# Scans that read one operand from PSUM, and products moved from VectorE to GpSimd, in a chunked linear attention with a routed expert stage

## The chip, the cores and the metric

The kernel runs on one core of one Trainium2 chip. The metric is the device time of one execution in microseconds. Its profile is of one execution; TensorE's clock there is given as a share of full speed, 2.4 GHz, so 0.50 is its lower level of 1.2 GHz.

## The reference, cut to what matters

A linear attention with a decaying state (4 batches, 8 heads, 768 steps, 48 dimensions) feeds a mixture of 8 experts over 3072 tokens of 384 values, each token going to the expert with the largest logit.

```python
for t in range(S):
    kt, vt, rt, wt = (k[:, :, t], v[:, :, t], r[:, :, t], w[:, :, t])
    cur = np.einsum('bhd,bhe->bhde', u[None] * kt, vt)
    y[:, :, t] = np.einsum('bhd,bhde->bhe', rt, state + cur)
    state = wt[:, :, :, None] * state + np.einsum('bhd,bhe->bhde', kt, vt)
...
x = y.transpose(0, 2, 1, 3).reshape(B * S, H * D)
logits = x @ w_gate
expert_idx = np.argmax(logits, axis=1)
...
    h = np.maximum(xe @ w1[e], 0.0)
    ye = h @ w2[e]
    out[mask] = gate_w[mask, None] * ye
```

## The kernel before

The first stage is the attention. Its 3072 tokens are 24 blocks: block n holds the 128 steps of chunk c of batch b, with n = 4c + b. Head pairs lie on 112 partitions (48 + 16 + 48), four pairs along the columns. `iteration(n)` (L739) runs for n = -3 to 21, and a hand-written end does blocks 22 and 23. Nothing reorders the instructions: each engine executes them as they are written, so an instruction that waits holds up all behind it on its engine.

One iteration has for a steady block n:

- **VectorE**: the running products of the decays forwards (`pre`, L367) and backwards (`suf`, L376) of block n+2, each one scan over four head pairs of 130 columns, 520 in all. Both multiply and add, and their added operand is an SBUF tile, `first` or `suf0`, that is zero but at the first column of each pair. Between them `reciprocal` (L370) writes the start of the backward scan. Then the products `rh` = r times pre (L349) and `kh` = k times suf (L385). `at` (L391) is two predicated copies of block n's scores from PSUM over the causal part of a tile that holds the diagonal.
- **GpSimd**: `rk` = r times k of block n+3 (L339; the first three blocks' on VectorE), held back by a dependency on the scan `pre` of block n+2; one diagonal of block n+1 (L355); and, from block 7 on, the indirect DMAs `xs<-xr,pi` (L679), four per chunk, that scatter 128 rows each to the expert that they are routed to. Their row numbers `pi` (L596) have three buffers.
- **TensorE**: the scores `ap` (L489), the state's part `yp<-rh,sst` (L501, from n = 4 on), the coefficients `cp` (L453, L456), transposes (L526, L480), the coefficients' transpose `yq<-pick,cs` (L461), the state `st` (L510), the values `yp<-at,vt` (L519).
- **ScalarE**: the copy of yp (`ytb`, in two halves L411 for the first four blocks, then in one L407), the state (L400), seven diagonals of block n+1 (L361), the coefficients `cs` of block n+2 (L422) that TensorE's L461 waits for, and smaller copies (L418, L440, L427, L396). L396 writes the carried decay into `first`.

Once per chunk there are also VectorE's gate (`mx`, `sh`, `oh`), a rank on TensorE, the exponentials on ScalarE and the count `seen` on GpSimd (L557). SyncE issues the loads; `rkwt` holds decays, r and k of a block (772 KB, six buffers).

`keep_warm(t, n)` (L118) issues n matmuls that nothing reads: 40 small and 12 wide ones at the start, 8 wide ones ahead of the coefficients of each of the first four blocks.

The second stage is the experts, sorted by size; `CAPS` are their padded row counts, in that order, in three or four groups of columns for the matmuls of L298 and in the last expert two groups of 128 rows and a rest. `Part` objects `pa` and `pb` are two halves of the first expert, computed while the attention ends; `mm1` expands, `mm2` contracts, `split_piece` and `feed` make the high and low parts of the next expert's weights, `load_x` starts a load of the next expert's rows `xg`.

Of the kernel before, what the change touches and what calls it, by code (L numbers as in the profile page):

```python
# [19 lines left out]
P = 128  # L20
# [5 lines left out]
WP = C + 2  # L26
NW = NP_ * WP
# [4 lines left out]
CAPS = (464, 440, 432, 408, 396, 384, 378, 360)  # L32
# [9 lines left out]
G0 = 2.0 ** 75  # L42
GMIN = 1e-28
# [3 lines left out]
BANK = 512  # L47
XC = DM + 2
# [4 lines left out]
def rwkv_moe_kernel(ctx, tc, rkw, vv, ub, wgp, wg, w1, w2, wc, out):  # L53
# [26 lines left out]
    def load(n):  # L80
# [9 lines left out]
        else:  # L90
# [3 lines left out]
            w=t[:, 0:NW], r=t[:, NW:NW + NR].rearrange("p (q c) -> p q c", c=C),  # L94
# [17 lines left out]
    wz = const.tile([P, BANK], BF16, name="wz")  # L112
# [222 lines left out]
    def mul_rk(n, eng):  # L335
        if real(n):
            d = blk[n]
            d["rk"] = wk.tile([RP, NP_, C], F32, name="rk", tag="rk", bufs=4)
            i = eng.tensor_tensor(out=d["rk"], in0=d["r"], in1=d["k"], op=ALU.mult)  # L339
            if real(n - 3):  # L340

                tc.add_manual_dep(i.ins, blk[n - 1]["prei"].name, mybir.DependencyInfo(
                    mybir.DependencyClass.Sync, mybir.DependencyReason.DATA), reason="beside the copies of the causal part")

    def dve_rh(n):
        if real(n):
# [16 lines left out]
    def dve_pre(n):  # L363
        if real(n):
            d = blk[n]
            pre = wk.tile([RP, NW], F32, name="pre", tag="pre")
            d["prei"] = nc.vector.tensor_tensor_scan(out=pre, data0=d["w"], data1=first[n % B].rearrange("p q c -> p (q c)"),  # L367
                                                     initial=0.0, op0=ALU.mult, op1=ALU.add).ins
            d["pre"] = pre.rearrange("p (q c) -> p q c", c=WP)
            d["rc"] = nc.vector.reciprocal(suf0[n % 2][:, :, WP - 1:WP], d["pre"][:, :, C:C + 1]).ins  # L370

    def dve_suf(n):
        if real(n):
            d = blk[n]
            suf = wk.tile([RP, NW], F32, name="suf", tag="suf")
            nc.vector.tensor_tensor_scan(out=suf[:, ::-1], data0=d["w"][:, ::-1],  # L376
                                         data1=suf0[n % 2].rearrange("p q c -> p (q c)")[:, ::-1],
                                         initial=0.0, op0=ALU.mult, op1=ALU.add)
            d["suf"] = suf.rearrange("p (q c) -> p q c", c=WP)
# [149 lines left out]
    def gate(k):  # L529
# [7 lines left out]
        nc.vector.tensor_single_scalar(out=oh, in_=sh, scalar=0.0, op=ALU.is_equal)  # L537
# [50 lines left out]
    def place(k):  # L588
# [5 lines left out]
        pi = sm.tile([P, B], I32, name="pi", tag="pi", bufs=3)[:, 0:m]  # L594
# [106 lines left out]
    class Part:  # L701
        def __init__(self, row, rows, t):
# [36 lines left out]
    def iteration(n):  # L739
# [40 lines left out]
        pe_y(n - 1)  # L780
        pe_kt(n + 1)
# [13 lines left out]
        if n == -1:  # L795
            mul_rk(2, nc.vector)
# [150 lines left out]
    with tc.manual_schedule(engines={ET.PE, ET.DVE, ET.Activation, ET.Pool}):  # L947
        for n in range(-3, NB - 2):
# [324 lines left out]
```

## Time and profile before

| | |
|---|---|
| median of the runs | 393.9 us (393.6 to 395.92, 3 runs) |
| the profiled execution | 394.28 us, of which the span is 392.5 |
| mean granted clock of TensorE | 0.989 |
| busy in the span | TensorE 373.4 us, VectorE 285.9, ScalarE 206.3, GpSimd 106.2 |

The span runs from the first to the last instruction, and what the execution has beyond it is 1.78 us. An engine that is busy 95% of the span on the mean can still wait in one stage, so the shares are read stage by stage. In rows of instructions "x2" means two of a kind in one row, and the bracket at the end is the idle time before them and what ended it.

### The profile page before, as it was taken

How to read it: one execution, taken by the hardware profiler on the slowest of the kernel's cores; microseconds unless marked ns; L12 is line 12 of the kernel's file. 1: busy time of each engine (PE TensorE's matmuls, PEld its weight loads, DVE VectorE, ACT ScalarE, POOL GpSimd, SP SyncE). 2: the span in 40 equal slices, each digit the busy share in tenths (PEclk: the TensorE clock that was granted, in tenths of full speed). 3: DMA queues.
4: the chain of work that ended last, by engine and by line, in shares of the span. 5: the costliest groups of instructions: out<-in, count | busy, mean ns of one | idle time of the engine just before them, and what ended most of it. 6: DMA issues, size and time to landing. Idle time of an engine off the chain costs nothing.

```text
span 392.5 us, 9368 instructions
## 1 busy us (share of the span) xinstructions
PE 373.4 (95%) x3545; PEld 339.8 (87%) x3548; DVE 285.9 (73%) x560; ACT 206.3 (53%) x559; POOL 106.2 (27%) x163
## 2 busy tenths in 40 slices
PE   8988999999999897999999999999999999999991
PEld 6567888878887777998999999999999999999991
DVE  7998999999999966888694693686693772722310
ACT  4788877877777655485443542463453541511200
POOL 2243256554656244111100330300240402102021
PEclk9999999999999899999999999999999999999997
DMA  8999868686706893499474475565366434001010
GB/s 287 407 304 286 254 218 262 203 253 186 251 28 169 301 306 134 139 282 265 138 227 160 125 258 186 161 193 217 120 190 214 128 114 155 21 0 46 11 37 24
DMA packets 32998, 71.25 MB, mean 182 GB/s; under 512 B 3972, under 2 KB 20229, under 8 KB 32946
## 3 DMA queue, kind: packets, MB, share of 16 engines
q1 hardware_dynamic: 29298, 61.11, 49.8%
q0 software_dynamic: 3648, 9.47, 6.6%
q8 instruction: 30, 0.49, 0.5%
q14 instruction: 22, 0.18, 0.1%
HBM read 58.73 MB, written 12.13 MB: 181 GB/s over the span
## 4 chain that ended last, share of the span: by engine, by line
PE 53%; DMA 2%; DVE 1%; issue 1%; ACT 1%; POOL 0%; POOLq 0%; SPq 0%; ACTq 0%; DVEq 0%
PE bank L298 23%; PE bank L921 14%; PE opt L315 12%; PE pt L289 2%; DMA xg<-xs 2%; PE op L910 1%; DVE w1l L235 1%; ACT w1h L233 0%; POOL out_dram L259 0%; DVE ot L911 0%; DVE ort L320 0%; ACT oT L928 0%; POOLq L1070 0%; DVE x L291 0%; ACT x L290 0%
## 5 line engine op out<-in xcount | busy, mean ns | idle before, releaser
L298 PE MATMUL bank<-xl,w1h 128*128 128x440 f32 (+6 forms) x168 | 58.2, 347 | 0.0
L298 PE MATMUL bank<-xh,w1l 128*128 128x440 f32 (+6 forms) x168 | 57.9, 344 | 0.0
L298 PE MATMUL bank<-xh,w1h 128*128 128x440 f32 (+6 forms) x168 | 55.4, 351 | 0.0
L361 ACT ACTIVATE at<-ident,cl 128x128 f32<-128x128 f32 x168 | 51.6, 392 | 0.0
L259 POOL DMA_INDIRECT out_dram<-ot,xg x16 | 21.3, 1332 | 103.2 <-DVE ot L911 99.5
L235 DVE TENSOR_TENSOR w2l<-wst,w2h 128x512 fp32r<-128x512 f32 x42 | 27.6, 687 | 24.6 <-ACT w2h L233 21.2
L300 ACT ACTIVATE hh<-bank 128x256 fp32r<-128x256 f32 (+8 forms) x58 | 26.7, 470 | 34.5 <-PE bank L298 31.5
L339 POOL TENSOR_TENSOR rk<-rkwt 112x512 f32<-112x512 f32 x21 | 27.1, 1289 | 56.3 <-DVE pre L367 49.5
L301 DVE SCALAR_TENSOR_TENSOR hl<-bank,hh 128x256 fp32r<-128x256 f32 (+8 forms) x58 | 30.0, 529 | 13.4 <-ACT hh L300 12.2
L259 POOL DMA_INDIRECT out_dram<-ort,xg x13 | 13.6, 1043 | 91.4 <-DVE ort L320 91.1
L391 DVE COPY_PREDICATED at<-cmask,ap 128x512 f32<-128x512 int32 x48 | 32.8, 740 | 1.3 <-PE ap L489 1.2
L298 PEld LDWEIGHTS bank<-xh,w1l 128*128 128x128 f32 x168 | 31.6, 188 | 0.5
L298 PEld LDWEIGHTS bank<-xl,w1h 128*128 128x128 f32 x168 | 31.6, 188 | 0.5
L233 ACT ACTIVATE w2h<-wst 128x512 fp32r<-128x512 f32 x42 | 24.5, 625 | 14.2 <-PE bank L921 10.0
L679 POOL DMA_INDIRECT xs<-xr,pi x24 | 27.5, 1147 | 16.2 <-DVE kh L385 3.4
L298 PEld LDWEIGHTS bank<-xh,w1h 128*128 128x128 f32 x168 | 31.4, 188 | 0.5
L367 DVE TENSOR_TENSOR_SCAN pre<-rkwt,first 112x520 f32<-112x520 f32 x24 | 29.6, 1233 | 0.9 <-DMA rkwt<-in_rkw_dram 0.9
L376 DVE TENSOR_TENSOR_SCAN suf<-rkwt,suf 112x520 f32<-112x520 f32 x24 | 29.9, 1244 | 0.0
L235 DVE TENSOR_TENSOR w1l<-wst,w1h 128x512 fp32r<-128x512 f32 x42 | 27.6, 687 | 1.7 <-ACT w1h L233 1.7
L489 PE MATMUL ap<-rh,kh 64*128 64x128 f32 (+1 forms) x384 | 28.4, 289 | 0.0
L315 PE MATMUL opt<-w2h,hh 128*128 128x384 f32 (+2 forms) x82 | 27.8, 345 | 0.0
L315 PE MATMUL opt<-w2h,hl 128*128 128x384 f32 (+2 forms) x82 | 27.7, 338 | 0.0
(168 smaller groups left out, 871.6 us busy)
## 6 DMA issues: line engine op xcount, KB each, us to landing
rkwt<-in_rkw_dram SPq DMA_DIRECT2D x23, 772.0 KB
wst<-in_w_dram SPq DMA_DIRECT2D x42, 256.0 KB
wst<-in_w_dram SPq DMA_DIRECT2D x14, 768.0 KB
vt<-in_vv_dram SPq DMA_DIRECT2D x24, 192.0 KB
wct<-in_wc_dram SPq DMA_DIRECT2D x24, 192.0 KB
xg<-xs SPq DMA_DIRECT2D x5, 579.0 KB
xs<-zrow SPq DMA_DIRECT2D x8, 289.5 KB
wsp<-in_w_dram SPq DMA_DIRECT2D x6, 256.0 KB
```

Of the source, the lines that this page charges most:

```text
L235: nc.vector.tensor_tensor(out=lo, in0=st[:, cs], in1=hi.bitcast(F32), op=ALU.subtract)
L259: i = nc.gpsimd.indirect_dma_start(out=out[:, :], out_offset=bass.IndirectOffsetOnAxis(ap=t.bitcast(I32)[:, q, DM + 1:DM + 2], axis=0), in ...
L298: nc.tensor.matmul(hp, a, x[:, j, :], start=(i == 0), stop=(i == 8))
L301: nc.vector.scalar_tensor_tensor(out=hl, in0=hp, scalar=0.0, in1=hh.bitcast(F32), op0=ALU.max, op1=ALU.subtract)
L315: nc.tensor.matmul(op, a[:, cs], w2v(wt, w, f), start=(i == 0), stop=(i == 23))
L361: nc.scalar.activation(blk[n]["at"][:, j, q], ident, AF.Copy, scale=blk[n]["ct"][:, 2 * q + j:2 * q + j + 1])
L367: d["prei"] = nc.vector.tensor_tensor_scan(out=pre, data0=d["w"], data1=first[n % B].rearrange("p q c -> p (q c)"), initial=0.0, op0=ALU.m ...
L376: nc.vector.tensor_tensor_scan(out=suf[:, ::-1], data0=d["w"][:, ::-1], data1=suf0[n % 2].rearrange("p q c -> p (q c)")[:, ::-1], initial= ...
L391: d["atc"] = nc.vector.copy_predicated(out=d["at"][:, j], mask=cmask.unsqueeze(1).broadcast_to([P, NP_, C]), data=d["ap"][j]).ins
L489: nc.tensor.matmul(d["ap"][j][:, q, :], d["kh"][rs, q, :], d["rh"][rs, q, :], start=True, stop=True)
L679: i = nc.gpsimd.indirect_dma_start(out=xsf, out_offset=bass.IndirectOffsetOnAxis(ap=ch["pi", c, b], axis=0), in_=xr[:, b, :], in_offset=No ...
L921: nc.tensor.matmul(pp, w, a, start=(i == 0), stop=(i == 23))
```

## The change

- The scans multiply and take a maximum. The second operand is one column of a PSUM bank that holds 2^-100, read for all columns (`floor`). The start of each pair now lies in the decays' own tile: a pair has 133 columns, 2^100, the start, 128 decays, the reciprocal, 2^100, so a scan has 533 columns. The tiles `first` and `suf0` and their memsets go.
- `rh` and every `rk` are GpSimd's. `rk` waits for the last `kh` issued (or the gate's `oh`), and not for `pre`. `rh` stands behind the diagonal and a scatter.
- The carried decay goes to `gend` on ScalarE, and a GpSimd copy of 112x4 (`pool_wt`) brings it into the decays' tile.
- On VectorE `at` stands ahead of `pre`. On ScalarE `cs` stands between the fourth and the fifth diagonal, and the exponentials behind them. `weigh` is later.
- The warm matmuls ahead of the coefficients: 6 for block 1, none for blocks 0, 2 and 3.
- `pi` has eight buffers.
- In the end of the attention, the splits of the second expert's weights and `load_x(1)` are written ahead of the two `pa.mm2`.
- The last cap is 368 for 360.

```diff
-WP = C + 2
-NW = NP_ * WP
+WP = C + 5
+NW = NP_ * WP + 4
...
-CAPS = (464, 440, 432, 408, 396, 384, 378, 360)
+CAPS = (464, 440, 432, 408, 396, 384, 378, 368)
...
+    for t in sacc:
+        nc.vector.memset(t[:RP, SC:SC + 1], 1.0 / UP)
+
+    def floor(n):
+        return sacc[n % B // 2][:RP, SC:SC + 1].broadcast_to([RP, NS])
...
-            if real(n - 3):
-
-                tc.add_manual_dep(i.ins, blk[n - 1]["prei"].name, mybir.DependencyInfo(
-                    mybir.DependencyClass.Sync, mybir.DependencyReason.DATA), reason="beside the copies of the causal part")
-
-    def dve_rh(n):
+            i = nc.gpsimd.tensor_tensor(out=d["rk"], in0=d["r"], in1=d["k"], op=ALU.mult)
+            if "behind" in ch:
+                tc.add_manual_dep(i.ins, ch.pop("behind").name, mybir.DependencyInfo(
+                    mybir.DependencyClass.Sync, mybir.DependencyReason.DATA), reason="not beside two inputs from SBUF")
+
+    def pool_rh(n):
...
-            d["prei"] = nc.vector.tensor_tensor_scan(out=pre, data0=d["w"], data1=first[n % B].rearrange("p q c -> p (q c)"),
-                                                     initial=0.0, op0=ALU.mult, op1=ALU.add).ins
-            d["pre"] = pre.rearrange("p (q c) -> p q c", c=WP)
-            d["rc"] = nc.vector.reciprocal(suf0[n % 2][:, :, WP - 1:WP], d["pre"][:, :, C:C + 1]).ins
+            nc.vector.tensor_tensor_scan(out=pre[:, 0:NS], data0=d["w"], data1=floor(n), initial=0.0, op0=ALU.mult, op1=ALU.max)
+            d["pre"] = pre[:, 0:NP_ * WP].rearrange("p (q c) -> p q c", c=WP)
+            nc.vector.reciprocal(d["wq"][:, :, C + 3:C + 4], d["pre"][:, :, C + 2:C + 3])
...
+    def pool_wt(n):
+        if real(n) and n >= B:
+            nc.gpsimd.tensor_copy(blk[n]["wq"][:, :, 2:3], gend[:, n % B, :].unsqueeze(2))
...
-        keep_warm(t, 8 if n < B else 0)
+        keep_warm(t, 6 if n == 1 else 0)
...
-        pi = sm.tile([P, B], I32, name="pi", tag="pi", bufs=3)[:, 0:m]
+        pi = sm.tile([P, B], I32, name="pi", tag="pi", bufs=8)[:, 0:m]
...
-        pa.mm2(0)
         split_piece(wts[1], stg[1, 0], 0)
         feed(1, 1, False)
-        pa.mm2(1, {f: [lambda j=j: pb.trans(j)] for j, f in enumerate((0, 2, 4))})
         split_piece(wts[1], stg[1, 1], 1)
         feed(1, 2, False)
         load_x(1)
+        pa.mm2(0)
+        pa.mm2(1, {f: [lambda j=j: pb.trans(j)] for j, f in enumerate((0, 2, 4))})
```

In the rows that follow, a scan is called SCALAR_TENSOR_TENSOR, and names are those of the code. VectorE, one iteration of the attention and the gate behind it, before:

```order
L367 SCALAR_TENSOR_TENSOR pre<-rkwt,first_165 112x520
L370 RECIPROCAL suf_0_176<-pre 112x4
L391 COPY_PREDICATED at<-cmask,ap 128x512 x2
L349 TENSOR_TENSOR rh<-rkwt,pre 112x512
L376 SCALAR_TENSOR_TENSOR suf<-rkwt,suf_0_176 112x520
L385 TENSOR_TENSOR kh<-rkwt,suf 112x512
L533 TENSOR_REDUCE mx<-cl 128x4
L535 TENSOR_TENSOR sh<-cl,mx 128x32
L537 TENSOR_SCALAR oh<-sh 128x32
```

The same place on VectorE in the changed kernel, where `st` is the PSUM bank with the column:

```order
L383 COPY_PREDICATED at<-cmask,ap 128x512 x2
L361 SCALAR_TENSOR_TENSOR pre<-rkwt,st_107 112x533
L363 RECIPROCAL rkwt<-pre 112x4
L369 SCALAR_TENSOR_TENSOR suf<-rkwt,st_107 112x533
L377 TENSOR_TENSOR kh<-rkwt,suf 112x512
L528 TENSOR_REDUCE mx<-cl 128x4
L530 TENSOR_TENSOR sh<-cl,mx 128x32
L532 TENSOR_SCALAR oh<-sh 128x32
```

The product rh has gone from between the two scans, and the predicated copies stand first. GpSimd, two iterations, the second with two scatters (the one-element memset stands behind each), before:

```order
L339 TENSOR_TENSOR rk<-rkwt 112x512
L355 AFFINE_SELECT at<-cl 128x128
L679 DMA xs<-xr,pi 24576x386
L688 MEMSET none 1x1
L339 TENSOR_TENSOR rk<-rkwt 112x512
L355 AFFINE_SELECT at<-cl 128x128
L679 DMA xs<-xr,pi 24576x386
L688 MEMSET none 1x1
L679 DMA xs<-xr,pi 24576x386
L688 MEMSET none 1x1
```

GpSimd in the changed kernel, from the copy that opens such an iteration to the next one:

```order
L391 COPY rkwt<-gend 112x4
L334 TENSOR_TENSOR rk<-rkwt 112x512
L349 AFFINE_SELECT at<-cl 128x128
L674 DMA xs<-xr,pi 24576x386
L683 MEMSET none 1x1
L343 TENSOR_TENSOR rh<-rkwt,pre 112x512
L674 DMA xs<-xr,pi 24576x386
L683 MEMSET none 1x1
L391 COPY rkwt<-gend 112x4
L334 TENSOR_TENSOR rk<-rkwt 112x512
```

The copy and rh have come in, with rh behind the first scatter and ahead of the second. ScalarE from the copy of yp to the carried decay, in one of the early iterations, before:

```order
L411 ACTIVATE ytb_196<-yp 48x512 x2
L400 ACTIVATE sst_191<-st_106 112x4x48
L361 ACTIVATE at<-ident,cl 128x128 x7
L422 ACTIVATE cs<-cp 128x128
L418 ACTIVATE xr<-yq 128x384
L440 ACTIVATE kt<-kbank 128x448
L427 ACTIVATE cl<-yq 128x16
L396 ACTIVATE first_166<-pre 112x4
```

The same stretch of ScalarE in the changed kernel:

```order
L406 ACTIVATE ytb_182<-yp 48x512 x2
L395 ACTIVATE sst_177<-st_106 112x4x48
L355 ACTIVATE at<-ident,cl 128x128 x4
L417 ACTIVATE cs<-cp 128x128
L355 ACTIVATE at<-ident,cl 128x128 x3
L413 ACTIVATE xr<-yq 128x384
L435 ACTIVATE kt<-kbank 128x448
L422 ACTIVATE cl<-yq 128x16
L387 ACTIVATE gend<-pre 112x4
```

The copy of the coefficients has come forward by three diagonals.

## Rows read from the trace of the kernel before

**Rows 1.** The page: the span, and VectorE's busy tenths in 40 equal slices.
```profile
span 392.5 us, 9368 instructions
...
DVE  7998999999999966888694693686693772722310
```

**Rows 2.** Windows, length; busy PE, PEld, DVE, ACT, POOL; clock, DMA share, GB/s.
```profile
13.78:42.01 28.23, 25.49 (x390) 19.52 (x391) 26.56 (x41) 22.76 (x74) 9.38 (x26) 1.00 0.98 312
42.01:111.92 69.91, 68.98 (x1204) 58.86 (x1202) 68.70 (x111) 54.30 (x186) 38.52 (x58) 1.00 0.69 220
111.92:140.00 28.08, 26.69 (x395) 21.52 (x393) 25.33 (x49) 19.35 (x65) 12.60 (x20) 0.94 0.61 191
```

**Rows 3.** Timeline of VectorE, one iteration: start, duration, line, operation.
```profile
53.01 1.23 DVE L367 TENSOR_TENSOR_SCAN pre<-rkwt,first 112x520 f32<-112x520 f32 x1
54.28 0.18 DVE L370 RECIPROCAL suf<-pre 112x4 f32<-112x4 f32 x1
54.39 1.39 DVE L391 COPY_PREDICATED at<-cmask,ap 128x512 f32<-128x512 int32 x2
55.67 0.74 DVE L349 TENSOR_TENSOR rh<-rkwt,pre 112x512 f32<-112x512 f32 x1
56.33 1.23 DVE L376 TENSOR_TENSOR_SCAN suf<-rkwt,suf 112x520 f32<-112x520 f32 x1
57.59 0.69 DVE L385 TENSOR_TENSOR kh<-rkwt,suf 112x512 f32<-112x512 f32 x1
58.20 1.24 DVE L367 TENSOR_TENSOR_SCAN pre<-rkwt,first 112x520 f32<-112x520 f32 x1
```

**Rows 4.** Timeline of ScalarE, one early iteration, 25.27 to 30.89.
```profile
25.27 1.20 ACT L411 ACTIVATE ytb<-yp 48x512 f32<-48x512 f32 x2 [0.28 <-PE yp L519]
...
29.51 0.49 ACT L418 ACTIVATE xr<-yq 128x384 f32<-128x384 f32 x1 [0.48 <-PE yq L461]
...
30.89 0.59 ACT L411 ACTIVATE ytb<-yp 48x512 f32<-48x512 f32 x1 [0.28 <-PE yp L519]
```

**Rows 5.** TensorE's waits from 28 to 40: total, times, longest.
```profile
PE yq L461 <- ACT cs L422: 2.4, 2, 1.2
```

**Rows 6.** Timeline of the start: VectorE's second scan, TensorE's warm matmuls.
```profile
8.76 1.24 DVE L367 TENSOR_TENSOR_SCAN pre<-rkwt,first 112x520 f32<-112x520 f32 x1 [0.65 <-DMA rkwt<-in_rkw_dram]
...
10.62 1.89 PE L118 MATMUL cp<-wz,ones 128*128 128x512 bf16 x8
```

**Rows 7.** Lines of GpSimd from 42 to 112 us: busy, mean ns, idle before.
```profile
L339 POOL TENSOR_TENSOR rk<-rkwt 112x512 f32<-112x512 f32 x13 | 16.8, 1291 | 31.7 <-DVE pre L367 28.0 <-ACT at L361 3.7
L679 POOL DMA_INDIRECT xs<-xr,pi x12 | 14.7, 1221 | 2.2 <-issue 2.2
L355 POOL TENSOR_SCALAR_AFFINE_SELECT at<-cl 128x128 f32<-128x128 f32 x13 | 3.8, 295 | 0.0
L557 POOL TENSOR_TENSOR seen<-seen,oh 128x32 bf16<-128x32 bf16 x3 | 2.0, 674 | 0.0
```

**Rows 8.** Timeline at 130 us: one count of GpSimd beside a scan.
```profile
129.86 1.23 DVE L367 TENSOR_TENSOR_SCAN pre<-rkwt,first 112x520 f32<-112x520 f32 x1
...
130.03 1.10 POOL L557 TENSOR_TENSOR seen<-seen,oh 128x32 bf16<-128x32 bf16 x1 [1.26 <-DVE oh L537]
```

**Rows 9.** Windows around TensorE's slower clock at the end of the attention.
```profile
135.00:137.00 2.00, 2.00 (x24) 1.39 (x22) 1.65 (x4) 1.22 (x6) 0.00 (x0) 0.50 0.80 266
```

**Rows 10.** TensorE's waits from 128 to 160 us.
```profile
PE rank L580 <- ACT ex L542: 2.4, 1, 2.4
PE yq L461 <- ACT cs L422: 1.1, 1, 1.1
```

**Rows 11.** VectorE's waits from 140 to 160 us.
```profile
DVE pi L596 <- DMA xs<-xr,pi: 1.0, 1, 1.0
```

**Rows 12.** TensorE's waits from 160 to 180 us.
```profile
PE pt L289 <- DMA xg<-xs: 0.4, 1, 0.4
```

**Rows 13.** TensorE by form from 300 to 384 us: the last expert's expansion.
```profile
L298 PE MATMUL bank<-xh,w1h 128*128 128x360 f32 x24 | 7.9, 330 | 0.0
```

More of the change, by code (lines that the diff above doesn't have):

```diff
@@ L47 @@
 BANK = 512
+SC = 2 * NP_ * D
+NS = NP_ * WP + 1
 XC = DM + 2
@@ L348, in dve_rh @@
             d["rh"] = wk.tile([RP, NP_, C], F32, name="rh", tag="rh", bufs=3)
-            nc.vector.tensor_tensor(out=d["rh"], in0=d["r"], in1=d["pre"][:, :, 0:C], op=ALU.mult)
+            nc.gpsimd.tensor_tensor(out=d["rh"], in0=d["r"], in1=d["pre"][:, :, 2:C + 2], op=ALU.mult)
     def pool_diag(n):
@@ L375, in dve_suf @@
             suf = wk.tile([RP, NW], F32, name="suf", tag="suf")
[L376 to L379, printed above, removed]
+            nc.vector.tensor_tensor_scan(out=suf[:, 0:NS][:, ::-1], data0=d["w"][:, ::-1], data1=floor(n), initial=0.0, op0=ALU.mult,
+                                         op1=ALU.max)
+            d["suf"] = suf[:, 0:NP_ * WP].rearrange("p (q c) -> p q c", c=WP)
     def dve_kh(n):
@@ L384, in dve_kh @@
             d["kh"] = wk.tile([RP, NP_, C], F32, name="kh", tag="kh", bufs=3)
-            nc.vector.tensor_tensor(out=d["kh"], in0=d["k"], in1=d["suf"][:, :, 2:WP], op=ALU.mult)
+            ch["behind"] = nc.vector.tensor_tensor(out=d["kh"], in0=d["k"], in1=d["suf"][:, :, 4:C + 4], op=ALU.mult).ins
     def dve_at(n):
@@ L536, in gate @@
         oh = sm.tile([P, B, E], BF16, name="oh", tag="oh")[:, 0:m]
-        nc.vector.tensor_single_scalar(out=oh, in_=sh, scalar=0.0, op=ALU.is_equal)
+        ch["behind"] = nc.vector.tensor_single_scalar(out=oh, in_=sh, scalar=0.0, op=ALU.is_equal).ins
         ch["r", k] = (sh, oh)
@@ L751, in iteration @@
         pe_a(n)
-        dve_pre(n + 2)
+        pool_wt(n + 2)
         act_state(n - 1)
-        if route >= 0 and b == 1:
-            act_ex(whole)
         if n >= 0:
-            mul_rk(n + 3, nc.gpsimd)
+            mul_rk(n + 3)
         pe_inter(n)
@@ L761, in iteration @@
         dve_at(n)
+        dve_pre(n + 2)
+        if n == -2:
+            nc.vector.tensor_reduce(out=pick, in_=ident.rearrange("p (q h) -> p h q", q=NP_)[:, 0:H + E, :], axis=AX.X, op=ALU.add)
         pool_diag(n + 1)
-        act_diag(n + 1)
+        act_diag(n + 1, slice(0, 4))
         if n >= 0:
             act_cs(n + 2)
+        act_diag(n + 1, slice(4, H))
+        if route >= 0 and b == 1:
+            act_ex(whole)
         for k in after.get(n, ()):
@@ L802, in iteration @@
             place(whole)
+            weigh(whole)
         pe_av(n)
@@ L1241, in rows @@
         return t
-    w = _np.zeros((NCH, B, RP, NP_, WP), inputs["w"].dtype)
-    w[..., 1:C + 1] = rows(inputs["w"], 1.0)
+    w = _np.zeros((NCH, B, RP, NW), inputs["w"].dtype)
+    wq = w[..., 0:NP_ * WP].reshape(NCH, B, RP, NP_, WP)
+    wq[..., 1] = wq[..., C + 4] = UP
+    wq[..., 2] = G0
+    wq[..., 3:C + 3] = rows(inputs["w"], 1.0)
+    w[..., 0:NP_ * WP] = wq.reshape(NCH, B, RP, NP_ * WP)
     rkw = _np.zeros((NB, P, NTP), w.dtype)
```

55 lines of the change are left out of this document (20 added, 35 removed).

## The prediction

> **What bounds the kernel now.** I read the page first: the span is 392.5 us, and VectorE's row of slices stands at 8 or 9 from the second to the fourteenth slice, and behind it reaches 9 in single slices only [rows 1]. So VectorE is full in the attention only, and the change, which takes work from VectorE, can act there. Next come windows cut at the starts of the scores `ap` of blocks 0, 5, 18 and 23 [rows 2], which give three stages with different bounds. In the first, 28.23 us for five iterations, TensorE is busy 25.49 (with warm matmuls among it) and VectorE 26.56: a period of 5.65 that no single engine fills. In the second, 69.91 us for thirteen iterations, TensorE is busy 68.98 and VectorE 68.70, so both are full: 5.31 an iteration of TensorE, the rank of each chunk included. Freeing VectorE there can give back no more than TensorE's idle 0.93. In the third, 28.08 us for five iterations, TensorE idles 1.39 and its mean granted clock is 0.94. From 180 us on the experts fill TensorE, so what the attention saves moves all that follows forward, and of the rest only the cap changes.
>
> VectorE's timeline shows the order of one iteration [rows 3]: from start to start the scan `pre` takes 1.27, the reciprocal 0.11, the copies `at` 1.28, `rh` 0.66, the scan `suf` 1.26, `kh` 0.61, together 5.19. ScalarE's timeline of an early iteration runs from 25.27 to 30.89, 5.62 with idle times of 0.48 and 0.28, so 4.86 of work [rows 4].
>
> **The change part by part.**
>
> *VectorE's iteration.* `rh` goes: 0.66. A scan of 533 columns for 520 is 1.27 x 533/520 = 1.30, and 1.29 for the backward one. No row shows a scan with a PSUM operand. The nearest is the predicated copy, whose data come from PSUM: two of 512 columns take 1.39, 0.70 each, against 0.69 for `kh` with both inputs in SBUF [rows 3]; so the operand adds between 0 and some 0.1, and I take 0.05 for each scan. The sum is 1.28 + 1.35 + 0.15 + 1.34 + 0.61 = 4.73 (4.6 to 4.85), with the reciprocal between its 0.11 and 0.18. That is 0.58 below TensorE's 5.31, so VectorE stops being a bound where the state is added, if nothing that GpSimd does now holds it up.
>
> *GpSimd's iteration.* Before, rk takes 1.29, and 31.7 us of idle time stand ahead of 13 of them [rows 7]. A chunk of four iterations now has four rk and four rh at 1.29 (10.3; rh has the same shape and engine), four diagonals at 0.295 (1.2), four scatters at 1.22 with 0.18 of issue (5.6), the count (0.7) and four copies of 112x4. For the copy the bounds are VectorE's reciprocal of 112x4 (0.18) and GpSimd's count of 128x32 (0.67) [rows 3, 7]; I take 0.25, since it has 4 columns and not 32. That gives 18.8 (18.5 to 20.5) against TensorE's 4 x 5.31 = 21.2. So GpSimd fits, at close to nine tenths. An iteration with two scatters needs 6.2 alone, but rh is made two blocks ahead of its use, and its neighbours need less than 5.
>
> *The start, −1.8.* VectorE's second scan at 8.76 waited for its load [rows 6], and this stays. TensorE's eight warm matmuls for block 1 run from 10.62 for 1.89, in front of its coefficients; six stay, and those for block 0 go. Behind the load come now rk(1) on GpSimd (1.29, to about 10), the coefficients, their copy and transposes, about 2: the first ap at 12.0 for 13.78. Bounds: only 0.5 is won (two warm matmuls at 0.24 each), or 2.4.
>
> *Blocks 0 to 4, −4.0.* The two bounds are now VectorE's 4.73 and, from block 1, ScalarE's 4.86 with its copies of yp in two halves. `cs` comes forward by three of seven diagonals, so TensorE's 2.4 us of waits for it, on two occasions [rows 5], should go. The five periods are 4.73 + 4 x 4.86 = 24.2 for 28.23. Bounds: 23.7 (VectorE alone), and 25.7 if a quarter us of the exchange with TensorE stays in each.
>
> *Blocks 5 to 17, −0.8.* TensorE's busy time is the floor, −0.93 at most, and 0 if GpSimd takes the slack.
>
> *Blocks 18 to 23, −2.3.* TensorE waits 1.1 for `cs` there [rows 10], and the clock then stands at 0.50 (the 1.2 GHz level) from 135 to 137 [rows 9]; a mean of 0.94 over 28.08 us is 1.7 us of lost clock. If wait and fall both go, 1.39 + 1.5 = 2.9 is won; if neither goes, nothing. With `cs` earlier and VectorE ahead I expect the wait to go and most of the fall with it.
>
> *The end of the attention, −0.9.* VectorE waits 1.0 for a buffer of row numbers, until scatters have landed [rows 11], and eight buffers end that. TensorE's rank idles 2.4 near it [rows 10], so the bounds are 0 and −2.4; the exponentials that the rank waits for still come, and I take 0.9.
>
> *Splits and load ahead of the two contractions, +0.3.* TensorE's wait of 0.4 for xg [rows 12] may go, since that load is issued earlier. On the other side, what takes the contractions' results out of PSUM now stands behind two more splits on ScalarE and VectorE, and the copies behind the transposes of `pb` with them. A split product is of the size of `kh`, 0.69 [rows 3]; one or two of them ahead of a result cost 0 to 1.2. Range −0.4 to +1.2.
>
> *The cap, +0.25.* The last expert's expansion has 72 matmuls of 360 columns at 330 ns [rows 13]. Eight columns more cost at most 8/360 of it each, 0.53 in all, and at least nothing; half.
>
> *At no cost:* the removed memsets and `weigh`, on engines that wait there; the reciprocal's new target; the exponentials behind the diagonals, two iterations ahead of need.
>
> **Sum.** −1.8 − 4.0 − 0.8 − 2.3 − 0.9 + 0.3 + 0.25 = −9.25. The profiled execution took 394.28, 0.4 above the median, so 385.0 there and **384.6** as a median.
>
> **The rivals.**
>
> *GpSimd becomes the bound (389).* rk now waits for the last `kh`, and `kh`, with both inputs in SBUF, could have to wait for an rh that is running. What speaks for it is one row: GpSimd's count takes 1.10 beside the scan that began at 129.86 and ended at 131.09, and itself ends at 131.13, against a mean of 0.67 [rows 7, 8]: two engines do hold each other up. Then rh, kh and the next rk stand in one chain, and GpSimd's 18.8 to 20.5 a chunk gets 4 x 0.61 on top: 21.2 to 22.9 against 21.2. With the middle, +1.0 a chunk over 4.25 chunks, it is 4.3 above the forecast. Against it: VectorE has 0.58 to spare in each iteration, and in those without a scatter rh ends before `suf` does.
>
> The Trainium skill, "SBUF — State Buffer", section "Who interferes with whom", says that a VectorE instruction with two SBUF inputs contends with a GpSimd instruction that reads SBUF, and one with at most one such input doesn't, and that whoever begins first holds the other up wholly. By its first half kh can stand behind rh, which is this rival; by its second half the scans against PSUM are free of rh, which is the forecast. The row of the count agrees with the first half; no row here has a scan with a PSUM operand.
>
> *The scans still stand behind GpSimd (405, slower).* Place: `suf` of every iteration, which VectorE wants to start while rh runs. If reading PSUM doesn't free the scan, it waits out most of the 1.29, say 1.2: an iteration of 4.73 + 1.2 = 5.93, with 0.55 of gate a chunk, so 23 iterations take 139 for the 126.2 of the three windows. With the gains of the start, the end and the costs, 394.28 + 12.9 − 1.8 − 0.9 + 0.55 = 405. It decides from a wait of some 0.7 an iteration on, where VectorE's 23 iterations take as long as before. For it: the count's row shows that such waits exist. Against it: rk beside the predicated copies, with one input in PSUM, has no longer mean (1.29) [rows 7] than elsewhere.
>
> *The early iterations don't gain (390.5).* They are paced by the exchange of ScalarE and TensorE and not by VectorE: ScalarE's idle times of 0.48 and 0.28 for TensorE remain [rows 4]. Then the start gives 1.0, blocks 0 to 4 give 0.5, the rest 0.8 + 1.0 + 0.9 − 0.55: −3.6. For it: no engine is full there. Against it: `cs` comes earlier, which is what TensorE waits for.
>
> **How the numbers follow.** The forecast has 0.58, GpSimd as the bound 0.18, no early gain 0.09, blocked scans 0.10, and 0.05 remain for what I don't see. With each term at its better bound the forecast would be −2.4 − 4.5 − 0.9 − 2.9 − 2.4 − 0.4 = −13.5, a median of 380.4, which is the low end, 380.5. The high end, 390.5, takes in GpSimd as the bound and the case without early gain; blocked scans lie outside, and so does the forecast with each term at its worse bound (−0.5 − 2.5 + 1.2 + 0.5 = −1.3). No change is within 1% of 393.9, 390.0 to 397.8. Faster: the forecast, two thirds of GpSimd as the bound, a third of the early case and most of the rest, 0.76. Same: 0.13. Slower: blocked scans and a little, 0.11.
>
> **What would show each step.** In the changed profile: `pre` and `suf` near 1.30 each, whether rh runs beside `suf` or not; at most one or two waits of kh behind rh; ap(0) near 12 and ap(5) near 36; TensorE without waits for `cs` before 40 us; TensorE's busy share of 98% or more between blocks 5 and 18; no wait for `pi`. I am wrong if the scans take 2 us or start late behind GpSimd, if GpSimd is busy over 95% in that stage with TensorE waiting for rh or rk, or if the clock falls in a new place, since fewer warm matmuls stand at the start.

## The result, and the profile after

The changed kernel takes 387.75 us median (387.55 to 388.52, 4 runs) for 393.75 (393.16 to 395.92, 4 runs): a ratio of 0.9841 (0.9802 to 0.9881). It is 6.0 us faster, where 9.2 was forecast. The page gives the shape: VectorE is lighter, and GpSimd is busy in the attention's slices, at up to eight tenths.

```profile
span 386.2 us, 9326 instructions
...
DVE  4999999898999868598784792895792853622310
...
POOL 4765588868767351102000510400320402112020
```

The windows are cut at the same places as in [rows 2], the starts of ap of blocks 0, 5, 18 and 23:

```profile
12.65:37.65 25.00, 23.42 (x375) 18.43 (x374) 24.45 (x33) 22.18 (x74) 16.18 (x35) 1.00 1.00 352
37.65:105.79 68.14, 68.14 (x1205) 58.63 (x1203) 63.80 (x100) 53.77 (x186) 52.70 (x86) 1.00 0.73 236
105.79:132.01 26.22, 24.86 (x395) 20.20 (x393) 24.59 (x46) 19.30 (x65) 16.13 (x27) 1.00 0.59 201
```

In the second window TensorE has no idle time left (68.14 of 68.14), VectorE has 4.34 and GpSimd 15.44. With the last rank of the attention at 152.96 before and 143.78 after, the spans divide so:

| stage | before | after | difference | forecast |
|---|---|---|---|---|
| to the first ap | 13.78 | 12.65 | −1.13 | −1.8 |
| blocks 0 to 4 | 28.23 | 25.00 | −3.23 | −4.0 |
| blocks 5 to 17 | 69.91 | 68.14 | −1.77 | −0.8 |
| blocks 18 to 22 | 28.08 | 26.22 | −1.86 | −2.3 |
| from there to the last rank | 12.96 | 11.77 | −1.19 | −0.9 |
| last rank to the end | 239.54 | 242.42 | +2.88 | +0.55 |

Up to block 23 the change wins 8.0 of the 8.9 that were forecast; behind the last rank 2.9 is lost again. The lines of VectorE between blocks 5 and 18 show what the scans cost now (mean ns behind the busy time; [rows 3] has single ones of before):

```profile
L369 DVE TENSOR_TENSOR_SCAN suf<-rkwt,st 112x533 f32<-112x533 f32 x14 | 17.7, 1264 | 0.5
L383 DVE COPY_PREDICATED at<-cmask,ap 128x512 f32<-128x512 int32 x26 | 17.7, 734 | 2.6 <-PE ap L484 2.5
L361 DVE TENSOR_TENSOR_SCAN pre<-rkwt,st 112x533 f32<-112x533 f32 x13 | 16.2, 1248 | 0.0
L377 DVE TENSOR_TENSOR kh<-rkwt,suf 112x512 f32<-112x512 f32 x13 | 9.5, 733 | 0.4
```

533 columns with a PSUM operand take what 520 took from SBUF, 1.25 for 1.23, and `at` waits for TensorE, 2.5 in all: VectorE has become the one that waits. GpSimd's lines of the same stretch answer to [rows 7]:

```profile
L334 POOL TENSOR_TENSOR rk<-rkwt 112x512 f32<-112x512 f32 x13 | 16.7, 1282 | 9.8 <-DVE oh L532 4.4 <-PE ap L484 3.7 <-DVE kh L377 1.8
L343 POOL TENSOR_TENSOR rh<-rkwt,pre 112x512 f32<-112x512 f32 x14 | 16.6, 1188 | 4.4 <-DVE pre L361 4.2
L674 POOL DMA_INDIRECT xs<-xr,pi x12 | 13.2, 1098 | 2.0 <-issue 1.6 <-DVE at L383 0.3
...
L391 POOL COPY rkwt<-gend 112x4 f32<-112x4 f32 x14 | 2.7, 193 | 0.0
...
L552 POOL TENSOR_TENSOR seen<-seen,oh 128x32 bf16<-128x32 bf16 x3 | 0.7, 236 | 0.0
```

The loss behind the last rank is in TensorE's waits there:

```profile
PE pt L284 <- DVE x L286: 2.1, 1, 2.1
PE rank L575 <- ACT ex L537: 1.4, 1, 1.4
```

VectorE's timeline names the cause. Six products of the splits stand in one row ahead of the copies `x`, which the next transpose waits for:

```profile
154.07 3.70 DVE L230 TENSOR_TENSOR w1l<-wsp,w1h 128x512 fp32r<-128x512 f32 x6 [0.82 <-ACT w1h L228]
...
158.70 0.65 DVE L286 TENSOR_TENSOR x<-pt,x 128x208 fp32r<-128x208 f32 x2
```

And the windows behind that wait show TensorE, idle from 158 to 159, granted half the clock from 160 on:

```profile
158.00:159.00 1.00, 0.00 (x0) 0.00 (x0) 0.89 (x4) 0.45 (x2) 0.00 (x0) 1.00 0.88 272
...
160.00:161.00 1.00, 1.00 (x5) 1.00 (x4) 0.31 (x1) 0.00 (x0) 0.03 (x1) 0.50 0.88 270
161.00:162.00 1.00, 1.00 (x5) 1.00 (x4) 0.00 (x0) 0.00 (x0) 0.00 (x0) 0.50 1.02 311
```

The fall at 135 us that [rows 9] show is not in this trace; the clock stands at 1.00 from 105.79 to 158. The mean over the span is 0.989 in both.

### The profile page after: what moved, and what is told of

Read it like the earlier page. It is cut to its first block, busy times and chain, and to the rows that moved or that the text cites. A ratio compares the mean times of both kernels' runs of the same rounds, so it can differ in the third digit from the quotient of the medians.

```text
span 386.2 us, 9326 instructions
## 1 busy us (share of the span) xinstructions
PE 368.3 (95%) x3522; PEld 338.5 (88%) x3522; DVE 273.6 (71%) x531; ACT 205.2 (53%) x559; POOL 134.2 (35%) x204
## 4 chain that ended last, share of the span: by engine, by line
PE 78%; DVE 9%; ACT 5%; issue 3%; DMA 2%; POOL 1%; SPq 1%; POOLq 0%; ACTq 0%; DVEq 0%
PE bank L293 28%; PE bank L920 14%; PE opt L310 13%; PE yp L496 4%; PE ap L484 4%; PE yp L514 3%; PE yq L521 2%; DVE at L383 2%; PE pt L284 2%; DVE pre L361 2%; PE st L505 2%; DMA rkwt<-in_rkw_dram 2%; PE kbank L475 1%; PE op L909 1%; ACT at L355 1%
## 5 line engine op out<-in xcount | busy, mean ns | idle before, releaser
L355 ACT ACTIVATE at<-ident,cl 128x128 f32<-128x128 f32 x168 | 53.8, 393 | 0.0
L334 POOL TENSOR_TENSOR rk<-rkwt 112x512 f32<-112x512 f32 x24 | 30.7, 1280 | 20.4 <-DMA rkwt<-in_rkw_dram 5.1
L343 POOL TENSOR_TENSOR rh<-rkwt,pre 112x512 f32<-112x512 f32 x24 | 28.9, 1205 | 12.0 <-DVE pre L361 10.8
L361 DVE TENSOR_TENSOR_SCAN pre<-rkwt,st 112x533 f32<-112x533 f32 x24 | 30.0, 1250 | 3.6 <-DMA rkwt<-in_rkw_dram 3.6
L369 DVE TENSOR_TENSOR_SCAN suf<-rkwt,st 112x533 f32<-112x533 f32 x24 | 30.3, 1264 | 0.8
L674 POOL DMA_INDIRECT xs<-xr,pi x24 | 25.3, 1053 | 14.0 <-DVE kh L377 3.8
L310 PE MATMUL opt<-w2h,hh 128*128 128x384 f32 (+3 forms) x82 | 28.2, 350 | 0.0
L310 PE MATMUL opt<-w2h,hl 128*128 128x384 f32 (+3 forms) x82 | 28.0, 343 | 0.0
```

The source lines that it names most:

```text
L310: nc.tensor.matmul(op, a[:, cs], w2v(wt, w, f), start=(i == 0), stop=(i == 23))
L334: i = nc.gpsimd.tensor_tensor(out=d["rk"], in0=d["r"], in1=d["k"], op=ALU.mult)
L343: nc.gpsimd.tensor_tensor(out=d["rh"], in0=d["r"], in1=d["pre"][:, :, 2:C + 2], op=ALU.mult)
L355: nc.scalar.activation(blk[n]["at"][:, j, q], ident, AF.Copy, scale=blk[n]["ct"][:, 2 * q + j:2 * q + j + 1])
L361: nc.vector.tensor_tensor_scan(out=pre[:, 0:NS], data0=d["w"], data1=floor(n), initial=0.0, op0=ALU.mult, op1=ALU.max)
L369: nc.vector.tensor_tensor_scan(out=suf[:, 0:NS][:, ::-1], data0=d["w"][:, ::-1], data1=floor(n), initial=0.0, op0=ALU.mult, op1=ALU.max)
```

## The experiments

**Theory.** The gain comes from VectorE's shorter iteration, which needs both rh on GpSimd and scans that GpSimd doesn't hold up; the loss comes from the order of the splits and the contractions. **Rivals:** the operand's place doesn't matter; rh doesn't matter; the loss is that of a shorter attention.

Runs e1 to e4, e5 to e8 and e9 to e11 were on three chips, where the kernel before took 395.15 (7 runs), 392.13 (a single run) and 394.13 (11 runs). Totals of different sets can thus differ by some 3 us with no edit, so across them the stages of the traces are compared: blocks 5 to 17 take 67.97 in e1 and 67.96 in e5 and e10.

### e1: contractions ahead of the splits again

```diff
+        pa.mm2(0)
         split_piece(wts[1], stg[1, 0], 0)
         feed(1, 1, False)
+        pa.mm2(1, {f: [lambda j=j: pb.trans(j)] for j, f in enumerate((0, 2, 4))})
         split_piece(wts[1], stg[1, 1], 1)
         feed(1, 2, False)
         load_x(1)
-        pa.mm2(0)
-        pa.mm2(1, {f: [lambda j=j: pb.trans(j)] for j, f in enumerate((0, 2, 4))})
```

> The changed kernel with the two contractions written ahead of the splits again, as in the kernel before. If the order alone gives back the 2.9 us that the changed profile loses between the third rank and the last copy of xg (a wait of 2.1 for VectorE's x, then 3.7 us at half clock), the median falls from 387.75 to 384.5 to 385.4, and the wait and the fall at 159 to 163 us are gone. If that loss comes from the shorter attention, which leaves the same splits less time, the median stays within 0.7 of 387.75 and the wait for x moves to another place.

385.32 us median, and on the same chip 395.15 for the kernel before: a ratio of 0.9756 (0.9734 to 0.9778) for the changed kernel's 0.9841. TensorE's waits from 130 to 190:

```profile
PE rank L575 <- ACT ex L537: 1.9, 1, 1.9
PE pt L284 <- DMA xg<-xs: 0.8, 1, 0.8
PE pt L284 <- DVE x L286: 0.3, 1, 0.3
```

The wait for x is 0.3, as it was before the change, and the clock is 1.00 through the contractions. From the last rank to the end this kernel needs 239.02 (143.88 to 382.9), so the order alone costs 3.4 us: 1.8 of a longer wait for x (2.1 for 0.3), and some 1.7 of half clock behind it. The wait for xg of 0.8 in these rows stands at 130.17, in block 22 and ahead of the last rank, and is for the first expert's rows. The wait of [rows 12], for the second expert's, has gone in both orders, so the earlier load isn't what ended it.

### e2: the kernel before with the splits first

The edit is the same move, the other way, in the kernel before.

> The kernel before with only the splits and the load written ahead of the two contractions. If the order alone costs it: the run takes 396 to 397 for 393.75, with a wait of TensorE for x near 168 us. If it costs only after a shorter attention: within 0.7 of 393.75.

397.59 in one run for 395.15, a little over the 396 to 397 expected. TensorE's longest wait, and one window of TensorE's clock behind it:

```profile
PE pt L289 <- DVE x L291: 2.2, 1, 2.2
```

```profile
170.00:171.00 1.00, 1.00 (x5) 1.00 (x4) 0.20 (x1) 0.00 (x0) 0.00 (x0) 0.50 0.99 342
```

The same wait of 2.2 and the same fall of the clock, in an attention that is not shorter: the order costs it alone. From the last rank to the end it takes 243.81 for 239.54; some 1.7 of these 4.3 is a second fall of the clock, behind the wait for the last rank (2.1), that the trace of the kernel before doesn't have.

The run shows one thing more, since its attention is that of the kernel before. The window from ap of block 18 to block 23:

```profile
112.44:138.99 26.55, 25.16 (x396) 20.32 (x394) 25.23 (x49) 19.34 (x65) 11.82 (x19) 1.00 0.55 189
```

It is 1.5 shorter than the 28.08 of [rows 2], with the same wait of 1.1 for cs in it and no fall of the clock. So the fall at 135 us belongs to one execution and not to the kernel, and against this trace the changed kernel's 26.22 wins 0.3 in that stage.

### e3: the scans' second operand in SBUF

```diff
+    flo = const.tile([RP, 1], F32, name="flo")
+    nc.vector.memset(flo, 1.0 / UP)
     def floor(n):
-        return sacc[n % B // 2][:RP, SC:SC + 1].broadcast_to([RP, NS])
+        return flo.broadcast_to([RP, NS])
```

> The changed kernel with the scans' second operand a column of SBUF and not of PSUM; nothing else moves. If the PSUM operand is what keeps the scans free of GpSimd's rh, suf takes or waits some 1.1 more in most iterations, VectorE's iteration is 5.7 to 5.9, and the run takes 395 to 404. If the place of the operand doesn't matter, 387 to 388.5 and suf stays at 1.26.

413.41 in one run for 395.15 of the kernel before: worse than either theory's number. Up to 3.4 of it is half clock from 15.1 to 21.9 us, which the changed kernel doesn't have. VectorE's lines from 40 to 120, and GpSimd's:

```profile
L372 DVE TENSOR_TENSOR_SCAN suf<-rkwt,flo 112x533 f32<-112x533 f32 x13 | 23.1, 1773 | 0.5
L364 DVE TENSOR_TENSOR_SCAN pre<-rkwt,flo 112x533 f32<-112x533 f32 x13 | 20.5, 1578 | 0.0
...
L380 DVE TENSOR_TENSOR kh<-rkwt,suf 112x512 f32<-112x512 f32 x14 | 16.4, 1172 | 0.5
```

```profile
L352 POOL TENSOR_SCALAR_AFFINE_SELECT at<-cl 128x128 f32<-128x128 f32 x13 | 13.5, 1035 | 0.0
L394 POOL COPY rkwt<-gend 112x4 f32<-112x4 f32 x12 | 8.6, 717 | 0.0
```

Every scan now costs 0.33 to 0.51 more on the mean, kh 0.44 more, and on GpSimd the diagonal 1.04 for 0.29 and the copy of 112x4 0.72 for 0.19. The hold goes both ways, and each one's delay puts the next into the other's way. Block 23 starts at 156.29 for 132.01. So the operand's place decides, and the rival on scans that stand behind GpSimd describes the kernel that this change would be without it; its price, 405, was too low, even without the half clock.

### e4: rh on VectorE again

```diff
-            nc.gpsimd.tensor_tensor(out=d["rh"], in0=d["r"], in1=d["pre"][:, :, 2:C + 2], op=ALU.mult)
+            nc.vector.tensor_tensor(out=d["rh"], in0=d["r"], in1=d["pre"][:, :, 2:C + 2], op=ALU.mult)
```

> The changed kernel with rh on VectorE again, behind pre; the scans keep their PSUM operand and GpSimd keeps rk. If VectorE's length sets blocks 0 to 4 and TensorE's idle of blocks 5 to 17, its iteration of 4.7 gets 0.6 longer, 5.3: about 2 us more to ap of block 5, 1.5 to 2 more from there to block 18, 391 to 392.5 in all. If the start and the order of cs made the gain and not rh, 387.5 to 388.5.

393.38 in one run (the kernel before 395.15 on that chip), over the 391 to 392.5 expected. The windows between ap of blocks 0, 5, 18 and 23:

```profile
12.04:38.17 26.13, 23.36 (x375) 18.61 (x374) 25.25 (x37) 22.28 (x74) 10.35 (x31) 1.00 1.01 359
38.17:107.65 69.48, 69.08 (x1205) 59.45 (x1203) 68.23 (x111) 54.41 (x185) 36.72 (x71) 1.00 0.70 225
107.65:136.39 28.74, 26.17 (x394) 20.80 (x394) 27.66 (x51) 19.07 (x66) 11.79 (x22) 1.00 0.58 185
```

VectorE is full again (68.23 of 69.48), and the three stages are 1.1, 1.3 and 2.5 longer than with rh on GpSimd. So rh on GpSimd is worth 5.0 from the first ap to block 23; the expectation had nothing for the last stage. That is its worth inside the changed order: in the last stage the old attention takes 26.55 in e2 with rh on VectorE. What remains of the gain in the first stage (28.23 to 26.13, 2.1) is not rh's; e7 finds the same 2.1 in the place of cs.

### e5 and e10: one cast on GpSimd

The profile of the changed kernel has one period between starts of ap that falls out of line, block 2 to 3, with 6.01 for 4.84 on both sides. VectorE's timeline and GpSimd's at that time, and one line each from the start:

```profile
12.57 1.68 DVE L377 TENSOR_TENSOR kh<-rkwt,suf 112x512 f32<-112x512 f32 x1
...
23.99 1.14 DVE L195 CAST ebrow<-ebase 1x32 bf16<-1x32 f32 x1
```

```profile
12.44 1.26 POOL L334 TENSOR_TENSOR rk<-rkwt 112x512 f32<-112x512 f32 x1
...
23.83 1.27 POOL L334 TENSOR_TENSOR rk<-rkwt 112x512 f32<-112x512 f32 x1
```

A cast of 32 values on one partition takes 1.14, and ends at 25.13, just behind the rk that began before it and ended at 25.10. kh of block 1, 1.68 for 0.69, ends at 14.25, 0.55 behind an rk that ended at 13.70. The same cast in the kernel before:

```profile
24.82 0.17 DVE L200 CAST ebrow<-ebase 1x32 bf16<-1x32 f32 x1
```

```diff
-        nc.vector.tensor_copy(ebrow, ebase[0:1])
+        nc.gpsimd.tensor_copy(ebrow, ebase[0:1])
```

on top of e1, and then the same kernel timed:

> The version with the contractions first, with the one cast of the expert bases (ebrow, 1x32) on GpSimd and not on VectorE. If the cast is held up by GpSimd's rk (1.14 us in the changed kernel, 0.17 in the kernel before), the period from ap of block 2 to block 3 falls from 6.0 to 5.0 and all later starts come 0.9 to 1.0 earlier, 383.7 to 384.5 in all. If something else sets that period, it stays at 5.8 to 6.0.

> The same kernel as the run with the cast on GpSimd, timed. If the 0.9 us of the cast is real, the ratio to the kernel before is 0.9725 to 0.9745; if that single run was a lucky one, 0.975 to 0.977 as without it.

The period of block 2 to 3 in the changed kernel, and then in e5:

```profile
21.42:27.43 6.01, 5.16 (x76) 3.79 (x74) 5.87 (x9) 4.72 (x16) 3.84 (x17) 1.00 0.98 307
```

```profile
21.64:26.50 4.86, 4.70 (x76) 3.67 (x74) 4.76 (x8) 4.72 (x16) 4.11 (x18) 1.00 1.03 313
```

4.86 for 6.01, as expected. e5 took 381.96 once (the kernel before 392.13 on that chip), less than the 383.7 expected; e10 has a median of 381.13 for 394.13, a ratio of 0.9675 (0.965 to 0.9699), lower than expected too. By the spans of the profiles e5 is 2.6 shorter than e1 (380.3 for 382.9): 0.9 is the cast (ap of block 5 at 36.72 for 37.62), and 1.6 a wait ahead of the last rank, 0.3 in e5 for 1.9 in e1. That second part isn't shown to be the cast's: e7 has it without the cast's move, and e6 tells more.

### e6: three buffers of row numbers

```diff
-        pi = sm.tile([P, B], I32, name="pi", tag="pi", bufs=8)[:, 0:m]
+        pi = sm.tile([P, B], I32, name="pi", tag="pi", bufs=3)[:, 0:m]
```

on top of e1.

> The version with the contractions first, with three buffers of row numbers again. If they were worth what the wait of before showed, VectorE waits 0.8 to 1.2 for pi near 142 us and the third rank of the end comes as much later, 385.5 to 386.5. If the rank waits for the exponentials anyway, nothing moves by more than 0.3.

387.26 in one run, over the 385.5 to 386.5 expected. VectorE's waits from 120 to 160, and TensorE's clock behind them:

```profile
DVE pi L591 <- DMA xs<-xr,pi: 1.9, 1, 1.9
```

```profile
147.00:149.00 2.00, 2.00 (x11) 2.00 (x11) 1.32 (x4) 0.98 (x3) 1.05 (x2) 0.50 0.00 0
```

From ap of block 23 to the last rank it takes 12.59; with eight buffers it is 10.71 in e5 and e7, but 11.77 in the changed kernel and 12.33 in e1. In those two pi waits for nothing; there ScalarE's copy of the second group of the expansion starts late, and the exponentials behind it. From ScalarE's timeline of e1:

```profile
142.07 0.38 ACT L295 ACTIVATE hh<-bank 128x256 fp32r<-128x256 f32 x1 [2.21 <-PE bank L293]
```

By TensorE's rows that group had ended at 140.41, but the trace has TensorE's signal for it only at 142.05, and the copy starts 0.02 behind the signal. In e5 the signal comes with the end (139.51 for 139.50). The copy is 1.1 to 1.7 late in the kernel before, the changed kernel and e1 to e4, and on time in e5 to e11, with the cast moved or not; why TensorE signals late isn't shown by the trace, and no run here settles it. So the buffers are worth 1.9 where the copy is on time (e6 against e5 and e7). Between the kernel before and the changed kernel the stage differs by 1.2, and the late copy, 1.1 in both, is no part of that.

Two falls of the clock add to e6, each some 1.7 at most: one behind an idle TensorE of 2.1 ahead of the last rank, and one in block 2, whose period is 6.82 for 5.99 in e1. e1, with an idle time of 1.9 ahead of that rank, had no fall there, and the kernel before, with 2.4, had none either.

### e7: cs behind all seven diagonals

```diff
-        act_diag(n + 1, slice(0, 4))
+        act_diag(n + 1)
         if n >= 0:
             act_cs(n + 2)
-        act_diag(n + 1, slice(4, H))
```

on top of e1.

> The version with the contractions first, with the copy of the coefficients behind all seven diagonals again. If its place made a part of the gain of blocks 0 to 4, TensorE waits 0.6 to 1.2 longer for it in each of blocks 1 to 3 and once or twice later, 386.5 to 388. If VectorE alone set those periods, within 0.5 of 385.3.

384.85 in one run (the kernel before 392.13 on that chip), so not 386.5: the total is a miss. The first window (blocks 0 to 4) and TensorE's waits from 8 to 132:

```profile
12.55:39.39 26.84, 22.43 (x375) 18.07 (x374) 24.12 (x34) 22.61 (x74) 16.89 (x36) 1.00 1.02 352
```

```profile
PE yq L456 <- ACT cs L417: 5.1, 6, 1.2
```

The mechanism is there: all periods of blocks 1 to 4 are 5.6, as before the change, and block 23 starts 1.8 later than in e1. The total hides it, as the last rank waited 0.3 here and 1.9 in e1, where the copy that e6 tells of was late; that copy is on time in e5 to e11 alike, so this isn't shown to be the order's doing. In the first stage cs is worth 2.1 (26.84 to 24.78 in e1), with the cast's 0.9 hidden in the long periods.

### e8: rk not held behind kh

The dependency of rk is taken out, on top of e1; nothing else.

> The version with the contractions first, where rk no longer waits for the last kh and may run beside it. If kh, with two inputs from SBUF, is held up by GpSimd, its mean goes from 0.73 to 1.2 or more between blocks 5 and 18, VectorE's iteration from 4.7 to 5.2 or more, and the run takes 386.5 to 392. If GpSimd's order leaves them apart anyway, within 0.5 of 385.3.

394.96 in one run, beyond the expectation and over the kernel before on that chip (392.13). VectorE's line of kh and TensorE's longest wait, which is for the diagonal on GpSimd:

```profile
L374 DVE TENSOR_TENSOR kh<-rkwt,suf 112x512 f32<-112x512 f32 x13 | 19.2, 1473 | 0.4
```

```profile
PE cp L445 <- POOL at L346: 5.3, 4, 1.3
```

kh doubles (1.47 for 0.73), and blocks 5 to 17 take 75.83 for 67.97. The rival of GpSimd as the bound is thus real as a mechanism, and the hold is what keeps it away: with it kh has 0.73 on the mean, 0.04 above an undisturbed one.

### e9: fewer warm matmuls

```diff
-WARM = (40, 12)
+WARM = (40, 6)
```

on top of e5.

> Contractions first and the cast on GpSimd, with 6 wide warm matmuls at the start and not 12. In the changed kernel the warm matmuls end at 8.4 us, 1.7 after rk of block 0 is there. If they hold up the coefficients of block 0, the first ap comes at 11.3 to 12.0 and not at 12.6, all that follows 0.6 to 1.2 earlier, and the run takes 0.6 to 1.2 less than the same kernel with 12. If the load or ScalarE's diagonals set the first ap, it stays within 0.3 of 12.6; if the clock falls for want of warm matmuls, some granted clock before 40 us is under 1 and the run is 1 or more longer.

TensorE's timeline of the start, in e9 and then in e10:

```profile
2.11 4.22 PE L121 MATMUL wb<-wz,ones 128*128 128x128 bf16 x44
7.29 0.43 PE L448 MATMUL cp<-rk,ubt 112*32 112x128 f32 x8 [0.97 <-POOL rk L334]
...
11.52 1.16 PE L484 MATMUL ap<-rh,kh 64*128 64x128 f32 x16
```

```profile
2.11 6.53 PE L121 MATMUL wb<-wz,ones 128*128 128x128 bf16 x50
8.56 0.43 PE L448 MATMUL cp<-rk,ubt 112*32 112x128 f32 x8
```

From the coefficients of block 0 to the first ap it is 4.2 in e9, e10 and the changed kernel (8.43 to 12.65), so their start sets it: with 12 they stand behind the warm matmuls, with 6 they wait for rk. The first ap comes 1.1 to 1.3 earlier, and behind the warm matmuls no granted clock is under 1 before 40 us. The time is 380.98 median, a ratio of 0.9687 (0.965 to 0.9723): the same as e10's 0.9675 within the intervals. The profiles differ by 1.4 in the span, but the same 50 warm matmuls took 6.53 in e10 and 5.59 in e11, whose first ap is at 11.84, so the gain over many runs may be half of it, and isn't shown.

### e11: the last cap at 360 again

The edit is the one number, on top of e5.

> Contractions first and the cast on GpSimd, with the last cap at 360 again. If the 8 columns cost what was forecast, the expansion of the last expert (68 matmuls before the last contraction) is 0.2 to 0.3 shorter than 11.4 us, and nothing else moves. If columns of that size cost nothing, it stays within 0.1.

381.42 in one run. The last expert's expansion takes 11.28 for 11.37 in e10 (347.15 to 358.43, 347.53 to 358.90), 0.09, and from the last rank to the end it is 238.94 for 238.99 in e10 and 238.90 in e9. The cap costs 0.1 at most, which is the second expectation.

No run separates the rest of the change: `at` ahead of `pre`, the later `weigh`, and smaller moves that the list of the change leaves out, such as the later tiles for the first expert's rows (`split_tiles`).

## Why the prediction was right, and where its terms were off

The time lies in the range and the sign and mechanism are those of the forecast; it wins two thirds of the size. The total alone would not have told it from the rival of GpSimd as the bound, whose 389 is nearer to 387.75 than 384.6 is. The trace does: between blocks 5 and 18 GpSimd is idle for 15.44 of 68.14 us and TensorE for none. Up to block 23 the sum of −8.0 for −8.9 holds some luck, in the start and in blocks 18 to 22.

- **VectorE's iteration** was given 4.73 and takes 4.65, from `at` at 29.67 to the next at 34.32. The PSUM operand was given 0.05 for each scan and costs nothing that shows.
- **GpSimd's iteration** was given 18.8 a chunk; 52.70 over 13 iterations is 16.2 of busy time. The count and the copy were taken too high (0.24 and 0.19 for 0.67 and 0.25), since the row for the count [rows 7] had itself been measured beside scans with two SBUF inputs, as [rows 8] show once. rh at 1.19 for 1.29 and the scatters at 1.10 for 1.22, with their issue counted as idle time, make up most of the rest.
- **The scans free of GpSimd:** right, shown by e3. The Trainium skill, "SBUF — State Buffer", section "Who interferes with whom", has the rule that divides the two cases by the number of SBUF inputs; the traces agree in both halves, suf beside rh at 1.26 with the PSUM operand and at 1.77 on the mean without. They agree for kh as well (0.73 held apart, 1.47 not).
- **The start, −1.8 for −1.13.** The step that failed is "behind the load come now rk(1) on GpSimd": the first ap hangs on the coefficients of block 0, which stand behind the start's own warm matmuls, and these were counted at nothing because they stood there before. The size is one draw: with 12 wide warm matmuls the first ap lies between 11.84 (e11) and 12.84 (e1), and with the start of the kernel before at 13.78 and 14.28 (e2).
- **Blocks 0 to 4, −4.0 for −3.23.** Blocks 1 and 3 have a period of 4.84 for ScalarE's 4.86, though that is no floor, as e9 has 4.73 to 4.75 in blocks 1 to 3. TensorE still waits for cs, 1.1 on four occasions from 10 to 40 us, where the forecast had none. Block 0 has 3.94 for 4.73 and block 4, which has the state's part, 5.38 for 4.86; these two nearly cancel. What is missing is the cast in block 2, 6.01 for 4.84, a line that the diff doesn't touch. The step that failed is that the sum left out what stood on VectorE once in that stage and runs beside GpSimd's rk now.
- **Blocks 5 to 17, −0.8 for −1.77.** The floor failed: TensorE's busy time of 68.98 was taken as fixed, and it is 68.14 now with the same matmuls. Part of what counts as busy was waiting inside: the 26 matmuls of the coefficients' transposes have a mean of 232 ns for 249, which is 0.44 of the 0.84. Where the rest lay isn't shown.
- **Blocks 18 to 22, −2.3 for −1.86.** The wait for cs went, as forecast, but a wait of 1.1 for kh ahead of the transposes of the expert's rows came in its place. What was won is the fall of the clock, and that is luck: e2 has the old attention without the fall and takes 26.55, so the part that belongs to the change is some 0.3. The step that failed is that the fall in one trace was taken as a cost of the wait for cs, of which the change would save most.
- **Row numbers, −0.9 for −1.19**, 1.9 by e6, where the copy of the second group is on time.
- **Splits first, +0.3 for +3.4.** This is the mis-sized term, and it holds most of the 3 us between forecast and time. The mechanism was named (copies behind the transposes stand behind splits), but priced at one or two products of 0.69; six stand there, 3.70. And the price of the wait was taken as the wait: the longer wait is 1.8 of the 3.4, and TensorE's clock at half speed behind it, which e1 has not, some 1.7 (0.77 from 159 to 160 in the changed kernel and 0.50 to 0.52 from there to 163). That the fall in [rows 9] had followed an idle TensorE had been used for the attention, and not here.
- **The cap, +0.25 for 0.1 at most.**

The version that beats both kernels is e10 (e9 within its interval): contractions first and the cast on GpSimd, 381.13 us at a ratio of 0.9675 to the kernel before, for the change's 0.9841. Of what it wins over e1 by the traces, about 1 is the cast's (0.9 in e5, 1.2 in e10) and 1.6 goes with the copy that is late in e1.

## What to carry to other kernels

When work moves from VectorE to GpSimd, list every VectorE instruction that will run beside it and ask of each where its operands lie: the long scans were freed by one PSUM operand, and a cast of 32 values then cost 1 us. When splits or other bulk work are written ahead of a contraction, count all of its products that stand ahead of the next small copy that TensorE waits for, and price the wait with the half clock that may follow it. Before a fall of the clock in one trace is written into a sum, look for it in a second execution. TensorE's busy time in a profile is no floor where its matmuls wait inside.

## What the runs showed of the hardware

- GpSimd and VectorE hold each other up in both directions: beside scans with two SBUF inputs GpSimd's diagonal takes 1.04 for 0.29 and its copy of 112x4 0.72 for 0.19, and the scans take 1.58 and 1.77 for 1.25 and 1.26 (e3).
- A VectorE cast with a single SBUF input was held as well, 1.14 for 0.17. The Trainium skill, "SBUF — State Buffer", section "Who interferes with whom", counts casts among the instructions that can take the shared pair of ports, in two-port modes that its rule on single SBUF inputs excepts and the prediction's sentence leaves out; the row agrees, though no run shows in which mode the cast ran.
- A scan with a PSUM operand that is one column read 533 times took 1.25, as a scan of 520 columns from SBUF (1.23).
- The same 50 warm matmuls took 6.53 in one run and 5.59 in another (e10, e11), and moved the first ap by 0.95. The windows give a granted clock of 1.00 there, but the 128 columns of the small ones start 107 ns apart at first, which is 1.2 GHz, and 56 ns apart later: the rise comes at 6.2 us in e10 and at 4.3 in e11.
- An idle time of TensorE of 2.1 to 2.2 ahead of the transposes was followed by half clock in all four traces that have it (the changed kernel, e2, e3 and e4). Ahead of the last rank, 2.1 was followed by it in e2 and e6, while 1.9 in e1 and e4 and 2.4 in the kernel before were not. One of 1.1 for cs was followed by it in the kernel before and not in e2. So in these traces the length of the idle time alone doesn't decide.
